# A pre-LN transformer block on one core: softmax without the row maximum, evacuations on VectorE, and a list-scheduled order

## The chip, the cores and the metric

The kernel runs on one core of one Trainium2 chip. The metric is the device time of one execution in microseconds (us). Times below are medians of several executions, with their range. Before the change the time was 1480.63 us (1480.35 to 1481.28, three runs).

Engines are named as in the profile: PE is TensorE (matrix products), PEld its weight loads, DVE is VectorE, ACT is ScalarE, POOL is GpSimd, SP is SyncE (it issues DMAs). `L1131` is a line of the kernel's source. The tile `pbank` in PSUM takes the results of the matmuls (`pbank<-...` in the traces); the kernels declare it as eight **banks** of 128x512 float32 each. A **dense** matmul is one of a projection or of the FFN, and **PV** is the product of the probabilities with the values.

## The reference

One block with S = 2048 tokens, D = 512, 32 heads of 16, and a gated FFN with F = 1792. All tensors are bf16, and the result may differ from the reference only by rounding. The code below is condensed by hand.

```python
def _A_ref(x, wqkv, wo):                       # attention, 32 heads of 16
    qkv = (x @ wqkv).reshape(B, S, 3, H, Dh).transpose(2, 0, 3, 1, 4)
    scores = einsum("bhqd,bhkd->bhqk", q, k) * (Dh ** -0.5)
    p = softmax(scores, axis=-1)
    return einsum("bhqk,bhkd->bhqd", p, v)...reshape(B, S, D) @ wo

def _B_ref(x, w_gate, w_up, w_down):           # gated FFN, tanh form of GELU
    return (gelu(x @ w_gate) * (x @ w_up)) @ w_down

h  = x + _A_ref(layernorm(x), A_wqkv, A_wo)
h2 = h + _B_ref(layernorm(h), B_w_gate, B_w_up, B_w_down)
```

The inputs are random with a scale of 0.05, so the scores are small numbers. That matters for a softmax that leaves out the maximum.

## The kernel before

Attention is cut into 32 **units**: 4 chunks of 512 queries times 8 slots of 4 heads. A unit has 32 ticks. In each tick TensorE makes two score tiles twice: once as queries x keys for the row maximum (pass 1, VectorE), and once transposed, as keys x queries with the negated maximum carried in extra rows, for the exponential (pass 2, ScalarE). The second pass runs one unit behind the first. Cuts are marked with `...`.

```python
def p1_pair(ui, j, gp, signal_last):                       # pass 1: scores for the maximum
    ...
    P.op("pe", lambda e, ...: e.matmul(pbank[:, b, :], QT[32*g:32*g+32, c, slot, 128*qt:128*qt+128],
                 KT[32*g:32*g+32, slot, 512*kc:512*kc+512], start=True, stop=True, tile_position=(32*g, 0)), ...)

def p1_consume(ui, tiles):                                 # 2048 of these, 128x512 each
    P.op("dve", lambda e, ...: e.tensor_reduce(out=PM[:, par, qt, kc, g:g+1], in_=pbank[:, b, :],
                                               axis=AX.X, op=ALU.max), ...)

def p2_consume(ui, tiles):                                 # 2048 of these, 128x512 each
    P.op("act", lambda e, ...: e.activation(out=PT[:, pi, :], in_=pbank[:, b, :], func=ACT.Exp), ...)

def evac_act(o_ap, i_ap, ...):                             # PSUM -> SBUF for projections, attention, FFN
    P.op("act", lambda e: e.activation(out=o_ap, in_=i_ap, func=ACT.Copy, **kw), ...)

def dummy(b, n):                                           # result is never read
    for i in range(n):
        P.op("pe", lambda e: e.matmul(pbank[:, b, :], ident[:], ones_bf[:, 0:512], start=True, stop=True), ...)

# ---- main loop, one pass per tick ----
    t1  = p1_pair(...)                     # 2 score matmuls for VectorE
    t2l = p2_pair(...)                     # 2 score matmuls for ScalarE
    p1_consume(...); p2_consume(...)
    pv_tick = p2_ok and (t2 % 4 == 1) and ...
    cost = 0 if pv_tick else dense.piece(deadline=dl)      # a piece (2 matmuls) of projection or FFN work
    if not pv_tick and (cost or 0) < 2 and p2_started:
        dummy(3 + p2_ring[0] % 3, 2 - (cost or 0))         # no dense work: multiply by ones instead
    if pv_tick:
        pv_burst(8)                        # probabilities x values
```

## Time and profile before

| quantity | before |
|---|---|
| time, median (range) | 1480.63 us (1480.35 to 1481.28) |
| span of the profiled execution | 1477.5 us |
| VectorE busy, ScalarE busy, TensorE busy | 88%, 87%, 75% |
| first exponential starts, last one ends | 94.6 us, 1411.5 us |
| tail after the last exponential | 66 us |
| start to start of two exponentials back to back, at best | 476 ns (each lasts 592 ns) |

The first fence holds lines of the profile's page of the kernel before. The first is busy time, share of the span and number of instructions of each engine. The second is the TensorE clock that the chip granted, in 40 equal slices, in tenths of full speed. The third is the share of the span that each engine holds in the chain of waits that ended last. The others are costly groups: line, engine, operation, output<-input, count, then busy us and mean ns of one, then the idle time before them and what ended it.

```profile
PE 1102.5 (75%) x8353; PEld 304.0 (21%) x8494; DVE 1301.6 (88%) x2159; ACT 1290.3 (87%) x2473; POOL 458.3 (31%) x593
...
PEclk9999999998999999999999999999999999999989
...
ACT 32%; DVE 31%; PE 19%; issue 16%; POOL 1%; DMA 1%; SPq 0%; POOLq 0%; ACTq 0%
...
L527 DVE TENSOR_REDUCE PM<-pbank 128x1 f32<-128x512 f32 x2048 | 1258.3, 683 | 70.7 <-PE pbank L568 56.2
L578 ACT ACTIVATE PT<-pbank 128x512 bf16<-128x512 f32 x2048 | 1117.8, 603 | 81.8 <-PE pbank L568 10.3
...
L810 PE MATMUL pbank<-ones_bf,ident 128*128 128x512 bf16 x756 | 239.9, 386 | 5.0 <-ACT PT L578 3.5
```

VectorE and ScalarE are both nearly full and share the chain. TensorE is not full, but it has 756 dummy matmuls, and its clock stands at full speed nearly throughout.

The second fence is from the timeline of the kernel before, in the middle of the run: start in us, length in us, then what ran.

```profile
700.43 0.39 PE L568 MATMUL pbank<-QT,KT 32*128 32x512 bf16 x2
...
700.75 0.61 PE L589 MATMUL pbank<-PT,VA 128*17 128x512 bf16 x8
...
701.29 0.39 PE L810 MATMUL pbank<-ones_bf,ident 128*128 128x512 bf16 x1
```

From the start of the score matmuls to the start of the next group is 0.32 us, and from the eight PV matmuls to the next group 0.54 us. Dense matmuls that follow each other are about 0.216 us apart; the score matmuls of a group start 3 ns apart, and so do four PV matmuls, with the next four some 0.21 us later. Each change of form costs about 0.1 us.

### The profile page before, as it was taken

To read this page: it belongs to the slowest core of one execution; us is meant where nothing else is said; L and a number is where in the kernel's file an instruction comes from. 1 tells how busy PE (TensorE), PEld (TensorE's weight loads), DVE (VectorE), ACT (ScalarE), POOL (GpSimd) and SP (SyncE) were. 2 spreads that over 40 slices of the span, in tenths; PEclk is the share of its full clock that TensorE was granted. 3 is DMA by queue.
4 is the path that set the end of the run, shared out by engine and by line. 5 is a ranking of instruction groups with operands and counts; after the bars stand their busy time and mean duration, and the time that the engine had idled before them with its cause. 6 is when DMAs were issued, how large, how long until landed. Compare 5 with 4: busy or idle time off the path is not lost.

```text
span 1477.5 us, 24601 instructions
## 1 busy us (share of the span) xinstructions
PE 1102.5 (75%) x8353; PEld 304.0 (21%) x8494; DVE 1301.6 (88%) x2159; ACT 1290.3 (87%) x2473; POOL 458.3 (31%) x593
## 2 busy tenths in 40 slices
PE   4977777776777777777887777777877777777869
PEld 2311111111112211111222211111222211111224
DVE  5989999998999999999999999999999999998023
ACT  3459999997999999999999999999999999999941
POOL 6000011110112245555212345554112345555130
PEclk9999999998999999999999999999999999999989
DMA  3000000013000000000000000000000000000000
GB/s 114 1 1 2 1 2 2 1 40 112 1 16 1 1 2 2 1 1 2 4 14 14 2 1 2 1 1 1 7 25 1 2 1 2 2 1 2 8 22 16
DMA packets 11531, 15.88 MB, mean 11 GB/s; under 512 B 1040, under 2 KB 9872, under 8 KB 11408
## 3 DMA queue, kind: packets, MB, share of 16 engines
q1 hardware_dynamic: 11408, 14.29, 2.9%
q8 instruction: 71, 1.16, 0.3%
q14 instruction: 52, 0.43, 0.1%
HBM read 11.80 MB, written 2.10 MB: 9 GB/s over the span
## 4 chain that ended last, share of the span: by engine, by line
ACT 32%; DVE 31%; PE 19%; issue 16%; POOL 1%; DMA 1%; SPq 0%; POOLq 0%; ACTq 0%
DVE PM L527 30%; ACT PT L578 27%; PE pbank L518 12%; PE pbank L794 2%; PE pbank L568 1%; PE pbank L462 1%; PE pbank L751 1%; ACT OA L440 1%; PE pbank L770 1%; ACT u_sb L440 1%; DVE stats L315 1%; ACT g_sb L440 1%; ACT sqj L682 0%; ACT OnT L440 0%; ACT QT L440 0%
## 5 line engine op out<-in xcount | busy, mean ns | idle before, releaser
L527 DVE TENSOR_REDUCE PM<-pbank 128x1 f32<-128x512 f32 x2048 | 1258.3, 683 | 70.7 <-PE pbank L568 56.2
L578 ACT ACTIVATE PT<-pbank 128x512 bf16<-128x512 f32 x2048 | 1117.8, 603 | 81.8 <-PE pbank L568 10.3
L518 PE MATMUL pbank<-KT,QT 32*128 32x512 bf16 x2048 | 399.5, 384 | 311.9 <-DVE PM L527 162.3
L568 PE MATMUL pbank<-QT,KT 32*128 32x512 bf16 x2048 | 398.1, 386 | 4.6 <-ACT PT L578 4.3
L518 PEld LDWEIGHTS pbank<-KT,QT 32*128 32x128 bf16 x2048 | 105.0, 91 | 776.3 <-DVE PM L527 767.6
L810 PE MATMUL pbank<-ones_bf,ident 128*128 128x512 bf16 x756 | 239.9, 386 | 5.0 <-ACT PT L578 3.5
L612 POOL TENSOR_TENSOR LINV<-OAT,negone 128x16 f32<-128x16 f32 x32 | 93.2, 2913 | 332.4 <-ACT OAT L440 332.4
L589 PE MATMUL pbank<-PT,VA 128*17 128x512 bf16 x2048 | 156.6, 383 | 0.0
L538 POOL CAST ST<-NEGM 128x16 bf16<-128x16 f32 x32 | 8.1, 252 | 358.1 <-DVE NEGM L532 358.1
L568 PEld LDWEIGHTS pbank<-QT,KT 32*128 32x128 bf16 x2048 | 96.2, 91 | 23.1 <-ACT PT L578 22.6
L729 POOL TENSOR_TENSOR w_sb<-g_sb 128x512 f32<-128x512 f32 x42 | 43.6, 1039 | 136.4 <-ACT g_sb L440 136.4
L810 PEld LDWEIGHTS pbank<-ones_bf,ident 128*128 128x128 bf16 x814 | 52.3, 97 | 110.6 <-ACT PT L578 96.4
L794 PE MATMUL pbank<-wd_sb,GUT 128*128 128x512 bf16 x214 | 57.0, 382 | 3.6 <-issue 1.0
L783 POOL TENSOR_TENSOR GUT<-th_sb,u_sb 128x512 bf16<-128x512 f32 x42 | 53.1, 1265 | 14.3 <-ACT u_sb L440 13.1
L802 DVE CAST out_sb<-pbank 128x512 bf16<-128x512 f32 x5 | 3.5, 692 | 61.2 <-PE pbank L798 61.2
L731 POOL TENSOR_TENSOR w_sb<-w_sb,g_sb 128x512 f32<-128x512 f32 x42 | 53.2, 1267 | 3.5
L735 POOL TENSOR_TENSOR th_sb<-th_sb,g_sb 128x512 f32<-128x512 f32 x42 | 53.2, 1266 | 3.5
L589 PEld LDWEIGHTS pbank<-PT,VA 128*17 128x17 bf16 x2048 | 28.3, 87 | 58.7 <-issue 58.4
L438 ACT ACTIVATE KT<-pbank,kbias 128x512 bf16<-128x512 f32 x32 | 22.1, 689 | 20.0 <-PE pbank L462 20.0
L462 PE MATMUL pbank<-xnT,wk_pad 128*128 128x512 bf16 x122 | 36.6, 415 | 1.9 <-issue 0.6
L462 PE MATMUL pbank<-xnT,wq_pad 128*128 128x512 bf16 x114 | 35.0, 383 | 2.3 <-issue 2.1
L734 POOL TENSOR_SCALAR th_sb<-th_sb 128x512 f32<-128x512 f32 x42 | 25.9, 618 | 28.6 <-ACT th_sb L741 28.6
(120 smaller groups left out, 749.7 us busy)
## 6 DMA issues: line engine op xcount, KB each, us to landing
x_sb<-in_A_x_dram SPq DMA_DIRECT2D x4, 512.0 KB, 5.6
QT<-STG SPq DMA_DIRECT2D x128, 3.0 KB
xres<-in_A_x_dram SPq DMA_DIRECT2D x16, 128.0 KB, 2.2
out_dram<-out_sb SPq DMA_DIRECT2D x16, 128.0 KB, 1.7
wg_sb<-in_B_w_gate_dram SPq DMA_DIRECT2D x1, 1792.0 KB, 7.1
wu_sb<-in_B_w_up_dram SPq DMA_DIRECT2D x1, 1792.0 KB, 11.2
wd_sb<-in_B_w_down_dram SPq DMA_DIRECT2D x1, 1792.0 KB, 16.8
wqkv_sb<-in_A_wqkv_dram SPq DMA_DIRECT2D x1, 1536.0 KB, 10.4
```

What stands on the lines that cost most here:

```text
L462: P.op("pe", lambda e, dc=dc: e.matmul(pbank[:, b, :], wp[:, dc, slot, :], xnT[:, dc, 512 * c:512 * c + 512], start=(dc == 0), stop=(dc == ...
L518: P.op("pe", lambda e, g=g, b=b: e.matmul(pbank[:, b, :], QT[32 * g:32 * g + 32, c, slot, 128 * qt:128 * qt + 128], KT[32 * g:32 * g + 32, ...
L527: P.op("dve", lambda e, b=b, qt=qt, kc=kc, g=g: e.tensor_reduce(out=PM[:, par, qt, kc, g:g + 1], in_=pbank[:, b, :], axis=AX.X, op=ALU.max ...
L568: P.op("pe", lambda e, g=g, b=b: e.matmul(pbank[:, b, :], KT[32 * g:32 * g + 32, slot, 128 * kt:128 * kt + 128], QT[32 * g:32 * g + 32, c, ...
L578: P.op("act", lambda e, b=b, pi=pi: e.activation(out=PT[:, pi, :], in_=pbank[:, b, :], func=ACT.Exp), reads=[("pb", b)], writes=[("PT", pi)])
L589: P.op("pe", lambda e, g=g, kt=kt, pi=pi, slot=slot: e.matmul(pbank[32 * g:32 * g + 17, PVB, :], VA[:, kt, 4 * slot + g, :], PT[:, pi, :], ...
L612: P.op("pool", lambda e: e.tensor_tensor(out=li, in0=oat4[:, :, :, 16], in1=negone[:].rearrange("p (q g) -> p q g", g=4), op=ALU.pow), rea ...
L731: P.op(eng, lambda e: e.tensor_tensor(out=ws, in0=ws, in1=gs, op=ALU.mult), reads=[("w", par), ("g", par)], writes=[("w", par)])
L735: P.op(eng, lambda e: e.tensor_tensor(out=ts_, in0=ts_, in1=gs, op=ALU.mult), reads=[("th", par), ("g", par)], writes=[("th", par)])
L783: P.op("pool", lambda e: e.tensor_tensor(out=GUT[:, fc, :], in0=ts_, in1=us, op=ALU.mult), reads=[("th", par), ("u", par)], writes=[("GUT" ...
L794: P.op("pe", lambda e, fc=fc: e.matmul(pbank[:, b, :], GUT[:, fc, 128 * qt:128 * qt + 128], wd_sb[:, fc, :], start=(fc == 0), stop=False), ...
L810: P.op("pe", lambda e: e.matmul(pbank[:, b, :], ident[:], ones_bf[:, 0:512], start=True, stop=True), reads=["ident", "ones_bf"], writes=[( ...
```

## The change

Intent: softmax does not need the maximum if the exponentials stay in range. So make the scores once, take the exponential directly, and check the sums at the end on chip: all 1/sum must lie between 1e-18 and 1e18. If one does not, the whole old algorithm runs behind a branch. That removes VectorE's main load, so the evacuations move from ScalarE to VectorE. Two exponentials merge into one of 128x1024. The order of all instructions comes from a list scheduler that works with a modelled duration for every operation.

The diff has about 2,100 lines. The old program stays in it as `max_path`. The core:

```diff
+# fast_path
+def qk():                                   # one step = two score tiles in two neighbouring banks
+    for st in range(NSTEP):                 # 1024 steps, two slots of two banks in turn
+        yield Op("pe", 0.25, [MM(pbank[:, bk[g % 2], :], KT[32*g:..., 128*kt:...], QT[32*g:..., c, slot, :],
+                                 True, True, (32*g, 0)) for g in (2*gp, 2*gp+1)],
+                 ..., gate=lambda: C["exp"] >= st - 1)
+def exps():
+    for st in range(NSTEP):
+        yield Op("act", 0.9, ACTF(PT[:, p0:p0+2, :], pbank[:, bk[0]:bk[0]+2, :], ACT.Exp), ...)
+def pv():                                   # every second step, four matmuls
+        yield Op("pe", 0.28, [MM(pbank[32*g:32*g+17, PVB, :], VA[:, kt, 4*slot+g, :], PT[:, p0+g, :],
+                                 kt == 0, kt == NT-1, (0, 32*g)) for g in range(4)], ...)
+def proj_kq(items):                         # dense pieces of two matmuls; FFN likewise
+    for hf in range(2):
+        yield Op("pe", 0.44, [MM(pbank[:, b, :], wp[:, dc, slot, :], xnT[:, dc, ...], dc == 0, dc == 3)
+                              for dc in (2*hf, 2*hf+1)], ...)
+    op = Op("dve", 0.61, lambda e, ...: e.tensor_copy(out=KT[...], in_=pbank[:, b, :]), ...)
+def check():                                # 1/sums in [1e-18, 1e18] -> flag == 128
+    ...
+        # every engine, at its end:
+            r = h.alloc_register("flag_" + name)
+            h.reg_load(r, flag[0:1, 0:1])
+            with h.If_ne(r, 128):
+                FP.run(name, h)             # max_path, the old algorithm
-    P.op("dve", lambda e, ...: e.tensor_reduce(out=PM[...], in_=pbank[:, b, :], axis=AX.X, op=ALU.max), ...)
-    P.op("pool", lambda e: e.tensor_tensor(out=li, in0=oat4[:, :, :, 16], in1=negone..., op=ALU.pow), ...)
-    dummy(3 + p2_ring[0] % 3, 2 - (cost or 0))
```

Only 26 dummy matmuls at the very start remain (`warm()`). An instruction still waits on its own engine's semaphore when it writes a bank that its own engine wrote last.

## The prediction

> **What bounds it now.** Span 1477.5 us; the profile's head shows VectorE busy 88%, ScalarE 87%, TensorE 75%. By costliest groups: the row-maximum reduction reads 2048 score tiles (128x512), 1258.3 us on VectorE; the exponential reads a second, transposed copy of the same scores in 2048 instructions, 1117.8 us on ScalarE. The chain of waits is shared: ScalarE 32%, VectorE 31%, TensorE 19%. In the trace two reductions start 598 ns apart, so one tick (two tiles of each pass) is about 1.2 us and 1024 ticks are 1225 us. Two exponentials fit in a tick with only ~0.2 us left for ScalarE's evacuations (about 170 us in all). First exponential at 94.6 us, last ends at 1411.5, then a 66 us tail.
>
> **Removed.** All 2048 reductions, 2048 score matmuls, maximum plumbing (32 transposes, copies, 128 small DMAs), 756 dummy matmuls, the 60 us of first pass before the first exponential, POOL's power with -1 (32 x 2.9 us). **Moved.** Projection, attention and FFN evacuations from ScalarE to VectorE: estimated from 0.69 us per evacuation, VectorE drops to about 250-300 us busy. **Merged.** Two exponentials become one of 128x1024: 1024 instructions. **Added.** 42 tanh remain on ScalarE; a tiny check and a branch on every engine; the old program, skipped (scores here are small, so I expect the branch not taken).
>
> **New bound: ScalarE's exponential stream.** Back-to-back 128x512 exponentials start 476 ns apart at best (592 ns each, overlapping), even when one carries an already satisfied wait. [...] 1024 steps = 925 us.
>
> Is TensorE in time? From the trace: exponential's end to score matmul 155 ns, matmul 390 ns, to the next exponential ~50 ns; with two slots a pair needs 1.02 + 0.6 = 1.62 us of 1.81, so ~0.19 us slack. A dense piece of two matmuls (0.43 us) fits between, so only occasional stalls.
>
> Sum (estimates):
> - start to first exponential 17 us
> - first unit, short of TensorE and VectorE time (projections, V, transposes ~38 us in a 29 us unit): 12 us of stall
> - exponentials 925, tanh 42 x 0.48 = 20
> - stalls of ScalarE from tanh waiting on POOL and from delayed score matmuls: 25
> - tail: ~62 (before 66; 28 gate/up groups of 0.86 us, four down groups of 3.0 us stay TensorE-bound; power of -1 leaves)
> - branch and offset between span and time: 3
>
> Total about 1064 us, i.e. -28%. Range 1035 to 1110. Chances: faster 0.97, same 0.01, slower 0.02.
>
> **What would show it.** Right: ScalarE busy over 88% and leading the chain (over 60%); exponential group 1024 x ~1.02 us, start-to-start 0.90; VectorE under 30%, TensorE 55-65%; first exponential near 17 us, last end near 1000. Wrong in a step: exponentials starting ≥0.95 us apart with "idle before" owed to the score matmul (slack missed) or to VectorE via a bank; ScalarE idle before tanh, released by POOL, over 10 us; tail over 70 us; first unit over 45 us.
>
> **What would make it wrong.** Without dummy matmuls TensorE's granted clock may fall below full in stretches without projection or FFN work: a score matmul then takes ~0.2 us longer, the slack is gone and each step grows (a few per cent; upper end of the range). The order is fixed ahead from modelled durations; where real latencies are longer, in-order waits on banks can cascade into ScalarE. A 1024-wide read across two PSUM banks costing more than estimated adds 10 us per 10 ns. If the check failed, the old program would run too: about 2500 us.

The sum is 17 + 12 + 925 + 20 + 25 + 62 + 3 = 1064 us. The 925 is 1024 steps of 0.903, and the kernel after shows that step: 903 ns from start to start at best, each 1018 to 1023 ns long. The clock that the last paragraph names as a risk is in the trace of after as well: 0.50 in the stretch 210 to 310 us, with 0.604 us for a score matmul in place of 0.384.

## The result, and the profile after

The time is 1198.99 us (1195.56 to 1202.32, four runs). The ratio to before is 0.810 (95% interval 0.8078 to 0.8121). Ratios here are the mean time of one kernel's fast runs over that of the other's in the same rounds, so they are not quite the ratio of the medians quoted. The kernel is correct and the branch is not taken. It is much faster, as predicted, but 135 us slower than the predicted time and 89 us above the top of the range.

The lines of the page of the kernel after that answer to those of before:

```profile
PE 1072.0 (90%) x5442; PEld 268.1 (22%) x5499; DVE 277.8 (23%) x478; ACT 1019.5 (85%) x1102; POOL 189.5 (16%) x194
...
PEclk9799998555799955555589955555569965555589
...
PE 65%; issue 14%; ACT 14%; DVE 2%; POOL 1%; ACTq 0%; DVEq 0%
...
L1131 ACT ACTIVATE PT<-pbank 128x1024 bf16<-128x1024 f32 x1024 | 983.5, 1023 | 99.0 <-PE pbank L1125 86.7
L1125 PE MATMUL pbank<-QT,KT 32*128 32x512 bf16 x2048 | 526.0, 519 | 80.7 <-ACT PT L1131 59.8
...
L1418 DVE SCALAR_TENSOR_TENSOR w_sb<-w_sb,g_sb 128x512 f32<-128x512 f32 x42 | 41.9, 999 | 7.4 <-ACT w_sb L1417 7.3
```

Three readings follow. First, TensorE does fewer matmuls than before (5442 against 8353) and yet is busy for 90% of the span and holds 65% of the chain; ScalarE, the predicted bound, holds 14%. (Some matmul records are missing from the trace; the weight loads, 5499 against 8494, are the better count.) Second, long stretches of the clock line read 5: TensorE ran at half speed there. Third, a score matmul takes 519 ns on average. Told apart in the trace, that is 0.384 us at full clock and 0.604 us at half clock.

Next, the windows view of the kernel after, three stretches: start:end and length in us, then busy us and number of instructions of each engine, the granted clock (PEclk, 1.00 is full), the DMA share and GB/s.

```profile
core 0: us, PE busy (x) PEld busy (x) DVE busy (x) ACT busy (x) POOL busy (x), PEclk, DMA share, GB/s
100.00:195.00 95.00, 92.51 (x552) 25.60 (x562) 35.34 (x55) 89.77 (x93) 0.00 (x0) 1.00 0.01 2
210.00:310.00 100.00, 87.96 (x425) 19.51 (x422) 5.39 (x12) 95.21 (x101) 0.00 (x0) 0.50 0.01 2
370.00:400.00 30.00, 28.16 (x166) 8.02 (x169) 11.62 (x17) 26.87 (x31) 9.64 (x9) 1.00 0.03 10
```

The first stretch has projections and full clock. The second is **quiet**, which here means that attention is the only work: half clock, with TensorE shown as 88% busy. The third is FFN work at full clock: TensorE is busy for 28.16 of 30 us. A high busy share alone doesn't make it the limit (it is 88% in the second stretch too); which wait holds ScalarE there is read from the timeline below.

Unit by unit, from the start of a unit's first exponential to that of the next unit (an ideal unit is 32 x 0.903 = 28.9 us):

| part | predicted | measured | difference |
|---|---|---|---|
| start to the first exponential | 17 | 26.0 | +9.0 |
| unit 0, above 28.9 | 12 | 18.6 | +6.6 |
| units 1 to 4 (projections), above 28.9 each | 0 | 15.4 | +15.4 |
| 18 quiet units, above 28.9 each | 0 | 49.6 | +49.6 |
| 9 units with FFN work, above 28.9 each (tanh 20 + stalls 25) | 45 | 88.8 | +43.8 |
| tail | 62 | 70.8 | +8.8 |
| sum | | | +133.2 |

So the spacing of the exponentials, 903 ns at best (925 us in all), is as predicted, and the miss is ScalarE waiting. In the profiled execution the sum accounts for the whole difference to the prediction (1195.56 - 1064 = 132; the prediction's last 3 us are for the branch and the offset between span and time).

Two places of the timeline show how ScalarE comes to wait. The first is a quiet unit of the kernel after:

```profile
242.33 0.61 PE L1125 MATMUL pbank<-QT,KT 32*128 32x512 bf16 x2 [0.55 <-ACT PT L1131]
...
243.25 0.61 PE L1125 MATMUL pbank<-QT,KT 32*128 32x512 bf16 x2 [0.31 <-ACT PT L1131]
243.79 0.60 PE L1125 MATMUL pbank<-PT,VA 128*17 128x512 bf16 x4
...
244.32 0.61 PE L1125 MATMUL pbank<-QT,KT 32*128 32x512 bf16 x2
```

With two slots, a slot's loop is the exponential (1.02), 0.16 to the score matmuls, 0.61 for them, and 0.05 to the next exponential: 1.84 us for two steps. Two steps of ScalarE need 1.81, so at half clock the slack is already gone. In one of two loops the score matmuls also stand behind a PV group (243.79), which holds them back by about 0.15 us more. The result is 1.98 us for two steps. At full clock the loop is 1.02 + 0.16 + 0.38 + 0.05 = 1.61 us and fits.

The second is a unit with FFN work, at full clock:

```profile
375.33 0.39 PE L1125 MATMUL pbank<-QT,KT 32*128 32x512 bf16 x2
...
375.65 0.40 PE L1125 MATMUL pbank<-PT,VA 128*17 128x512 bf16 x4
...
375.98 1.27 PE L1124 MATMUL pbank<-hnT_c_70,wu_sb 128*128 128x512 bf16 x4
...
376.64 0.11 PEld L1124 LDWEIGHTS pbank<-hnT_c_70,wu_sb 128*128 128x128 bf16 x2 [0.55 <-PE pbank L1124]
377.18 0.10 PEld L1125 LDWEIGHTS pbank<-QT,KT 32*128 32x128 bf16 x4 [0.42 <-ACT PT L1131]
...
377.61 1.02 ACT L1131 ACTIVATE PT<-pbank 128x1024 bf16<-128x1024 f32 x1 [0.52 <-PE pbank L1125]
```

Score to PV is 0.32 us and PV to dense 0.33 us. Then two dense pieces stand directly behind each other, and the second waits for the first to end: the weight load at 376.64 is released by PE itself. The four matmuls take 1.27 us, and the next exponential starts 0.52 us after ScalarE had become free. Across the trace a dense pair costs 0.54 us (median) until the next group starts, not 0.43.

The start is the third place, again from the timeline of the kernel after:

```profile
1.74 17.28 PE L1486 MATMUL pbank<-ones_bf,ident 128*128 128x512 bf16 x26 [1.74 <-POOL ident L1156]
...
12.53 0.56 DVE L1175 COPY wk_pad<-wqkv_sb 128x1536 bf16<-128x1536 bf16 x1 [3.00 <-DMA wqkv_sb<-in_A_wqkv_dram]
...
16.08 8.27 POOL L1214 TENSOR_SCALAR xn_sb<-x_sb,mv,rstd 128x512 bf16<-128x512 bf16 x4 [0.19 <-POOL rstd L1209]
```

Each of the 26 warm-up matmuls waits for the one before (0.667 us each, modelled as 0.25) and so they hold TensorE until about 19 us. On VectorE a copy waits 3.00 us for a load before it can start, and so does what stands behind it. POOL's four normalisations take 2.07 us each, modelled as 0.77. In before four of the same shape took 0.77 us, but these multiply and add, and after's subtract and multiply; VectorE is not the reason, since the first of the four took 2.09 us with VectorE idle throughout.

### The profile page after: what moved, and what is told of

Read it like the earlier page. It is cut to its first block, busy times and chain, and to the rows that moved or that the text cites. A ratio compares the mean times of both kernels' runs of the same rounds, so it can differ in the third digit from the quotient of the medians.

```text
span 1193.7 us, 14797 instructions
## 1 busy us (share of the span) xinstructions
PE 1072.0 (90%) x5442; PEld 268.1 (22%) x5499; DVE 277.8 (23%) x478; ACT 1019.5 (85%) x1102; POOL 189.5 (16%) x194
## 4 chain that ended last, share of the span: by engine, by line
PE 65%; issue 14%; ACT 14%; DVE 2%; POOL 1%; ACTq 0%; DVEq 0%
PE pbank L1125 39%; PE pbank L1124 20%; ACT PT L1131 13%; PE pbank L1323 3%; PE pbank L1365 2%; DVE OA L1319 1%; POOL xn_sb L1214 1%; PE pbank L1359 0%; PE pbank L1381 0%; ACT w_sb L1417 0%; ACTq L152 0%; DVE stats_93 L1372 0%; DVE w_sb L1418 0%; DVE QT L1254 0%; DVE h_c_69 L1368 0%
## 5 line engine op out<-in xcount | busy, mean ns | idle before, releaser
L1131 ACT ACTIVATE PT<-pbank 128x1024 bf16<-128x1024 f32 x1024 | 983.5, 1023 | 99.0 <-PE pbank L1125 86.7
L1125 PE MATMUL pbank<-QT,KT 32*128 32x512 bf16 x2048 | 526.0, 519 | 80.7 <-ACT PT L1131 59.8
L1125 PE MATMUL pbank<-PT,VA 128*17 128x512 bf16 x2048 | 270.1, 519 | 0.8 <-ACT PT L1131 0.6
L1323 PE MATMUL pbank<-ident_79,OA 128*128 128x128 f32 x128 | 38.9, 401 | 6.5 <-DVE OA L1319 5.7
L1418 DVE SCALAR_TENSOR_TENSOR w_sb<-w_sb,g_sb 128x512 f32<-128x512 f32 x42 | 41.9, 999 | 7.4 <-ACT w_sb L1417 7.3
L1407 DVE COPY g_sb<-pbank 128x512 f32<-128x512 f32 x42 | 29.0, 690 | 35.9 <-PE pbank L1124 35.8
L1443 DVE SCALAR_TENSOR_TENSOR GUT<-pbank,w_sb 128x512 bf16<-128x512 f32 x42 | 29.0, 691 | 24.5 <-PE pbank L1124 23.2
L1410 POOL TENSOR_SCALAR w_sb<-w_sb 128x512 f32<-128x512 f32 x42 | 30.5, 726 | 3.7
L1257 DVE CAST KT<-pbank 128x512 bf16<-128x512 f32 x32 | 22.1, 691 | 31.6 <-PE pbank L1124 31.6
L1365 PE MATMUL pbank<-wo_sb,OnT 128*128 128x512 bf16 x57 | 24.9, 529 | 2.6 <-issue 1.7
L1417 ACT ACTIVATE w_sb<-w_sb 128x512 f32<-128x512 f32 x42 | 26.3, 626 | 0.0
## 6 DMA issues: line engine op xcount, KB each, us to landing
wu_sb<-in_B_w_up_dram SPq DMA_DIRECT2D x1, 1792.0 KB, 11.8
```

The costliest lines, as they stand in the source:

```text
L1125: return lambda e: e.matmul(o, l, r, start=start, stop=stop, tile_position=tile)
L1131: return lambda e: e.activation(out=o, in_=i, func=func, **kw)
L1323: yield Op("pe", 0.44, [lambda e, qt=qt: e.transpose(out=pbank[:, b, 128 * qt:128 * qt + 128], in_=OA[:, par, 128 * qt:128 * qt + 128], id ...
L1365: yield Op("pe", 0.44, [lambda e, hc=hc: e.matmul(pbank[:, b2, :], OnT[:, qt, hc, :], wo_sb[:, hc, :], start=(hc == 0), stop=(hc == 3)) fo ...
L1407: yield Op("dve", 0.61, lambda e: e.tensor_copy(out=gs, in_=pbank[:, b, :]), reads=[("pb", b)], writes=[("g", i)], extra=dE)
L1410: yield Op("pool", 0.62, lambda e: e.tensor_scalar(out=ws, in0=ws, scalar1=GA, scalar2=1.0, op0=ALU.mult, op1=ALU.add), reads=[("w", i)], ...
```

## The experiments

Three theories at the outset:

- **Clock:** without dummies TensorE falls to half clock in the quiet units, and this lengthens the loop beyond ScalarE's time. Holding the clock gives the time back.
- **Groups and self-waits:** at full clock TensorE is still late, because a change of matmul form and TensorE's waits on its own semaphore cost time that the scheduler's model leaves out.
- **POOL (rival):** in the FFN units ScalarE's tanh waits for the three POOL operations of GELU.

15 kernels ran. "Quiet units" are the 18 units without dense work, `QUIET = [5, 6, 7]` and the last five of each later chunk. A run of a program on one core is labelled slow when it is more than 1.5% above the fastest of the same kernel; here every such run shows a lower mean clock than the fast ones of its kernel (spreadT 0.81 and 0.85 against 0.91 to 0.92). The profiles of fill2noself, spread, spreadfill and spreadT are of executions labelled slow: unit times quoted for them hold for those executions, and the fast ones may have lost the clock in other places. Ratios are to the kernel before, of fast runs only. They ran in four groups (1 to 4, 5 to 8, 9 to 12, 13 to 15), each on one chip of its own; the kernel before measured about 1480 us in each.

### 1. fill2: two dummy matmuls per two steps in the quiet units

```diff
                 C["pv"] = n
+                if u in QUIET and kt % 1 == 0:
+                    b = yield Acquire(reads=["ones_bf", "ident"])
+                    yield Op("pe", 0.44, [MM(pbank[:, b, 0:512], ident[:], ones_bf[:, 0:512], True, True)] * 2, ...)
+                    sch.release(b)
```

> Two 128x512 dummy matmuls (identity times ones, into a free bank) after each PV group in the 18 units that have no projection or FFN work; the order on ScalarE, VectorE and POOL is unchanged. Theory A (clock): those units run at granted clock 0.5, where the loop exponential - score matmul - exponential takes 1.02+0.16+0.61+0.05 = 1.84 us per pair plus 0.15 us behind a PV group, so 0.99 us per step; with the clock back at 1.0 these units fall from 31.7 to 29.0-29.5 us, the units after them start warm, in all -45 to -65 us (about 1135-1150 us). Rival B (in-order waits on TensorE, whatever the clock): extra TensorE work can only lengthen the step; same or up to 30 us slower.

Measured: 1153.98 us (1143.42 to 1154.46), ratio 0.7774 (0.7737 to 0.7812), clock 0.952 on average against 0.70. ScalarE, VectorE and POOL have the same instructions in the same order as after. The clock line of the page of fill2, then from its windows view a quiet stretch and an FFN stretch:

```profile
PEclk9899999699999979999989979999989979999989
...
250.00:300.00 50.00, 42.21 (x269) 11.87 (x274) 1.41 (x4) 50.00 (x56) 0.00 (x0) 1.00 0.00 1
360.00:390.00 30.00, 28.19 (x163) 7.70 (x166) 14.61 (x20) 26.82 (x31) 14.34 (x13) 1.00 0.01 5
```

TensorE has more matmuls than in the quiet stretch of after (5.4 per us against 4.25), is busy for less of the time (84% against 88%), and ScalarE is busy for 50.00 of 50 us. A quiet unit takes 29.6 us in place of 31.7. The gain has two halves. The 18 quiet units together save 20 us, because each group's first one still starts at half clock (33.5 to 34.9 us). The units that follow them, 8, 16 and 24, no longer start at half clock and save 19 us (37.6, 43.3, 43.1 become 33.2, 36.1, 36.1). Units 9 and 10 do not change. The clock theory is confirmed for some 45 us, and its rival (more TensorE work can only lengthen a step) is out. The first unit of a group pays for the change: unit 11 takes 33.6 us where it took 31.4, since it has the dummies before it has the clock.

### 2. fill1: half the dose

The same edit with one matmul in place of two.

> The same with one dummy matmul per PV group (half the dose). Theory A: if one is enough to hold the clock, the same gain as with two, -45 to -65 us; if the clock stays at 0.5 in those units, the extra matmul (0.43 us at half clock) delays every second score matmul and it is 10-60 us slower. Rival B: between 0 and 15 us slower, with no jump.

Measured: 1267.8 us (1262.63 to 1272.68), ratio 0.8578. The windows view of fill1, a quiet stretch:

```profile
260.00:300.00 40.00, 36.18 (x167) 8.42 (x166) 1.37 (x3) 33.73 (x37) 0.00 (x0) 0.50 0.00 1
```

The clock stays at half, and the dummy is now pure cost: +69 us, with quiet units at 34.8 to 36 us. This is the outcome that was named for a clock that stays at half, and more than the 10 to 60 us expected for it. So there is no smooth trade: 0.22 us of extra streaming per two steps (at full clock) did not hold the clock, 0.43 us did. TensorE is 90% busy in this stretch and is still not given the full clock.

### 3. noself: TensorE does not wait for itself

The waits on TensorE's own semaphore are left out. The result was correct in the run.

```diff
-            if k == e.name and v > e.count:
+            if k == e.name and (v > e.count or k == "pe"):
                 continue
```

> TensorE's waits on its own semaphore are left out ([...]inside a group there were none before either). Order of all engines unchanged. Theory: the second half of each dense piece waits for the first half's drain (0.55 us against 0.43 us of work), so back-to-back halves lose ~0.2 us; in the tail 24 of them fall: gates and ups 2.04 us per pair to 1.75, tail -4 us; in the FFN units 2-4 us per unit, 9 units; in all -15 to -35 us. Rival: halves seldom stand back to back outside the tail, so only the tail's 4-5 us come.

Measured: 1170.48 us (1165.76 to 1179.61), ratio 0.7924. The tail falls from 70.8 to 60.7 us, unit 9 from 40.5 to 38.6, and quiet units from 31.7 to 31.1. The self-waits cost about 27 us, within the 15 to 35 expected, but not where they were expected. In the profiles 10 us are in the tail and 13 in the 18 quiet units, which run at half clock; the nine FFN units, for which 2 to 4 us each were expected, give back 2.5 us together, because units 18 and 26 lost the clock for a while (34.4 became 37.2 and 35.7). The self-waits account for the miss in the tail.

### 4. nopool: POOL's GELU made almost empty

Wrong (relative error 0.024): the three POOL operations work on one column, and tanh reads another tensor.

```diff
-        yield Op("pool", 1.05, lambda e: e.tensor_tensor(out=ws, in0=gs, in1=gs, op=ALU.mult), ...)
+        yield Op("pool", 1.05, lambda e: e.tensor_tensor(out=ws[:, 0:1], in0=gs[:, 0:1], in1=gs[:, 0:1], op=ALU.mult), ...)
         ... (the other two likewise)
-        yield Op("act", 0.5, lambda e: e.activation(out=ws, in_=ws, func=ACT.Tanh, scale=GC), ...)
+        yield Op("act", 0.5, lambda e: e.activation(out=ws, in_=gs, func=ACT.Tanh, scale=GC), ...)
```

> Wrong results on purpose: POOL's three GELU operations work on 1 column instead of 512, tanh reads the gate values directly; order and waits unchanged. Rival C (the FFN units, 34-43 us against 28.9, are held by POOL's chain, which runs 1.19+0.73+1.35 us instead of 1.04+0.62+1.27, and by VectorE's slowed SBUF operations): each FFN unit falls by 4 us or more, in all -35 us or more. Theory A2 (FFN units are held by TensorE: dense pieces cost 0.54 us not 0.43 and push the score matmul past its slack): less than 8 us in all.

Measured: 1200.68 us (1194.36 to 1201.84), ratio 0.8104, the same as after. The FFN units are unchanged (37.6, 40.4, 34.4 us). POOL is not the limit, and this rival is out. (The start and unit 0 took 6 us more in this profile, at a lower clock: the third slice of its clock line is 8, in after 9.) One line changed, in the groups view of nopool:

```profile
L1418 DVE SCALAR_TENSOR_TENSOR w_sb<-w_sb,g_sb 128x512 f32<-128x512 f32 x42 | 28.8, 686 | 7.4 <-ACT w_sb L1417 7.3
```

This VectorE operation took 999 ns on average in after (679 to 1796) and takes 686 ns in nopool, where POOL is nearly idle. Overlap with POOL alone does not set the time: some of those in after took under 700 ns with POOL busy beside them almost throughout.

### 5. fill2narrow: FFN matmuls of half the width

fill2, with gate, up and down matmuls of 256 columns. Its output is wrong, which doesn't matter for the time. If TensorE's time in the FFN units is the limit, they should shrink.

```diff
-                yield Op("pe", 0.44, [MM(pbank[:, b, :], wg_sb[:, dc, ...], hT[:, dc, :], dc == 0, dc == 3)
+                yield Op("pe", 0.44, [MM(pbank[:, b, 0:256], wg_sb[:, dc, ...], hT[:, dc, 0:256], dc == 0, dc == 3)
```

> Wrong results on purpose, on top of fill2 (clock held): gate, up and down matmuls stream 256 columns instead of 512; order and waits unchanged. Theory A2 (the second FFN unit of each chunk, 40.4 us, is held by TensorE's own streaming: 85 dense matmuls x 0.216 + scores and PV 10.4 us + ~80 changes of group x 0.1 us = 37 us): it falls by about 85 x 0.108 = 9 us to 31-32 us, the third unit from 34.4 to 29.5-30.5, and the tail by 10-18 us; in all -45 to -65 us against fill2 (about 1090-1105 us). Rival (latency of waits between engines, not streaming): the second unit falls by less than 4 us.

Measured: 1196.96 us (1196.09 to 1198.27), ratio 0.8086: 45 us slower than fill2, not 45 to 65 faster. The windows view of fill2narrow, the same place as the second line of fill2 above:

```profile
360.00:400.00 40.00, 38.91 (x173) 9.26 (x171) 15.82 (x24) 29.31 (x34) 19.44 (x18) 0.50 0.00 1
```

With less work to stream, TensorE fell to half clock in units 9 and 10 and they took 51.3 and 44.1 us in place of 40.4 and 34.4. The experiment cannot answer the question it was made for, and whether TensorE's own streaming is the limit of the FFN units stays without a test. It shows something else: with less work for TensorE the kernel became slower, and the units that grew are those where the clock went.

### 6. fill2noself: both together

> fill2 and noself together, to see whether they add up. If independent: fill2's 1149 us less 15-25 us (tail -10, FFN units -1.5 each; the 0.6 us per quiet unit that noself gained at half clock is not there at full clock): 1125-1135 us. If noself's gain came through the clock, only the tail's 10 us: 1140 us.

The edits of 1 and 3. Measured: median 1139.3 us; one fast run of 1118.86 at clock 0.964, and three labelled slow (1137.5 to 1141.2, clock 0.933 to 0.941), so there is no ratio. In the profiled run quiet units take 29.4 us, unit 9 38.4, and the tail 60 us. Against fill2's mean of 1151.5 the fast run gains 33 us and the others 10 to 14, so the two gains add up in one run of four only. The profile shows where it goes: units 17, 18, 25 and 26, which held the full clock in fill2, now dip below it (0.97 and 0.91; 40.1 and 37.2 us for the first two). Why they dip is not shown.

### 7. spread: the scheduler gets measured durations

noself, with the durations that the trace showed and a guard that keeps a dense piece from starting if it would delay the next score matmuls by more than 0.15 us. No dummies.

```diff
+EXTRA = dict(pe=0.06, act=0.19, dve=0.09, pool=0.05)     # from an operation's end to its user
+SLACK = 0.15
-            yield Op("pe", 0.25, [MM(...)])               # score group;  PV 0.28 -> 0.33, dense 0.44 -> 0.54
+            yield Op("pe", 0.33, [MM(...)])
+            qr = self._qk_due()                           # when the next score matmuls can start
+            if "pe" in best and qr < self.INF: ...        # push a dense piece that does not fit behind them
```

> noself, and the list scheduler given the measured durations (score group 0.33, PV 0.33, dense pair 0.54 us) and a guard: a dense pair may not start when it would end more than 0.15 us after the next score group is due; so FFN work spreads over 7 units per chunk (10-38 dense matmuls per unit, before 85 in one). No dummies. Theory A2: no unit after the first is over 32 us, FFN units 29.5-31 at full clock; [...] in all 1065-1090 us. Rival (total work, not its bunching): the units' sum stays, about 1165 us as noself.

Measured: 1204.94 us (1186.71 to 1227.32; the two fast ones average 1194.4), ratio 0.807. Expected were 1065 to 1090, so this missed by over 100 us. Against noself (fast mean 1171.8), which it contains, it is 23 us slower. Two stretches of the windows view of spread:

```profile
120.00:240.00 120.00, 117.02 (x465) 21.36 (x472) 18.64 (x30) 96.73 (x95) 0.00 (x0) 0.50 0.00 1
470.00:520.00 50.00, 43.33 (x265) 11.45 (x270) 12.72 (x20) 50.00 (x58) 14.63 (x15) 1.00 0.00 1
```

Both stretches have about 28 dense matmuls per unit, evenly spread. In the first, units 2 to 5 run at half clock throughout and take 40.6 us each. In the second the clock is full, ScalarE is busy for 50.00 of 50 us, and the units take 29.3 to 31.6 us. The even order does what it was made for, but only at full clock. A load of about 28 dense matmuls per unit can stay in either state for over 100 us, so the number of matmuls alone does not decide. Whether the state in which it was entered does, or the order within the units, no run isolates.

### 8 to 10. spreadfill, spreadT, spreadTP: dummies only where TensorE would be slack

spreadfill adds a dummy pair after a PV group if no dense pair ran since the PV group before:

```diff
+                if C["warm"] and C["dense"] == C["dense0"]:
+                    b = yield Acquire(reads=["ones_bf", "ident"])
+                    yield Op("pe", 0.54, [MM(pbank[:, b, :], ident[:], ones_bf[:, 0:512], True, True)] * 2, ...)
```

> As spread, with a pair of dummy matmuls after a PV group whenever the last period had no dense pair (never more than one pair per period). Theories A and A2 together: every unit after the first at 29.3-30.3 us at clock 0.95 or more; 26 us start + 46 first unit + 31 x 29.8 + 61 tail = 1050-1065 us. If the clock costs nothing once the work is spread: the same as spread.

Measured: 1178.53 us (1149.77 to 1198.26; fast mean 1158.3), ratio 0.7826. Missed (1050 to 1065 expected). In the profile the clock is at 0.58 to 0.73 in units 4 to 6, 8, 14 to 16, 22 to 24, 26, 28 and 31. The working guess was that transposes are the cause, since the edit counts a transpose group as dense work and leaves the dummies out there. The profile does not show it: every unit has transposes, and units 3 and 4 have nearly the same matmuls, one at full clock and one at 0.58.

spreadT does not count transposes, puts a 256-column dummy matmul ahead of each group of them, and adds a dummy pair only where no dense work is waiting:

```diff
-        yield Op("pe", 0.5, [lambda e, hc=hc: e.transpose(out=pt[...], in_=Otok[...], identity=ident[:]) for hc in range(4)], ...)
+        yield Op("pe", 0.60, [MM(pbank[:, b, 0:256], ident[:], ones_bf[:, 0:256], True, True)]
+                           + [lambda e, hc=hc: e.transpose(...) for hc in range(4)], ...)
```

> As spreadfill, but a transpose group no longer counts as a dense pair (in spreadfill it suppressed the dummies, and its periods had no 512-column matmul) and carries one 256-column dummy itself; a dummy pair comes only when no dense work waits. So every PV period (1.8 us) has about two full matmuls or one half-wide one. Theory A3 [...]: clock 0.93 or more, units after the first 29.3-31 us, in all 1050-1080 us. Rival: the clock is unstable at this load whatever the gaps: 1130 us or more.

Measured: 1125.63 us (1119.58 to 1198.52; three of five fast, mean 1122.0), ratio 0.7566. Expected were 1050 to 1080: missed. In the profile, of a slow execution (1171.01), the later units are mostly at full clock, but units 2 to 5 still take 40.9 us at half clock. The fast runs have a clock of 0.91 to 0.92 against 0.85; where they lost it was not profiled.

spreadTP also mends the start: LayerNorm on VectorE in place of POOL, longer landing times of the loads in the schedule (6 to 9 us) and the warm-up matmul at 0.43 us.

> spreadT with the start reordered: real landing times of the loads in the schedule, the normalised input on VectorE instead of POOL, the warm-up dummies modelled at their real 0.43 us. Expected: first exponential at 18-22 us instead of 26-32, first unit 40-46 us, so -8 to -15 us against spreadT if the clock does the same in both.

Measured: 1181.68 us (1167.81 to 1209.12; fast mean 1170.9), ratio 0.7982: some 49 us slower than spreadT, where 8 to 15 us less were expected. The first exponential comes at 27.5 us in place of 32.0, but the clock was at or near half in units 2 to 5 again and in 16, 17, 24 and 25 as well (0.55 to 0.67). So a small shift at the start came with a different set of units that lose the clock. The four runs with the new order agree on one thing: as long as the clock was lost somewhere, the gain of the order was not reliable.

### 11. zeropv: other matmuls in place of the dummies

Which matmuls keep the clock: only dummies of the form 128\*128, as in fill2, or others that stream for as long? Eight more PV-shaped matmuls (form 128\*17) with zero weights after each PV group in the quiet units, accumulating zeros. In the trace of before eight PV matmuls take 0.54 us until the next group, as a dense pair does, so they are taken to stream for 0.43 us, like fill2's pair.

```diff
-                                      for g in range(4)],
+                                      for g in range(4)]
+                         + ([MM(pbank[32*g:32*g+17, PVB, :], zw[:, 0:17], PT[:, p0+g, :], False, False, (0, 32*g))
+                             for g in range(4)] * 2 if u in QUIET and kt < NT - 1 else []),
```

> Change as it came, plus after each PV group of the quiet units two more PV-shaped groups with zero weights (17 columns in each of 4 column groups): the same 0.43 us of streaming per period as fill2, in narrow matmuls. If the clock follows streaming time: as fill2, -45 us (1150). If it follows the share of the array in use: clock stays 0.5 and the extra groups (0.86 us at half clock) hold up the scores: +40 to +80 us (1240-1280).

Measured: 1162.84 us (1160.62 to 1164.75), ratio 0.7851, clock 0.941. A quiet stretch in its windows view:

```profile
250.00:280.00 30.00, 24.18 (x258) 7.29 (x260) 1.38 (x3) 29.76 (x33) 0.00 (x0) 1.00 0.01 1
```

It holds the clock nearly as well as fill2 (0.952); in the profile it lost it once in unit 8, which takes 44.9 us in place of 33.2, about the 11 us that lie between the means of the two. So neither the form 128\*128 nor non-zero weights were needed: 0.43 us more of streaming per two steps was enough in either form, and fill1's 0.22 was not.

### 12. evacact: evacuations back on ScalarE

fill2, with 185 evacuations on ScalarE as before the change.

```diff
-        yield Op("dve", 0.61, lambda e: e.tensor_copy(out=OA[:, par, :], in_=pbank[:, PVB, :]), ...)
+        yield Op("act", 0.5, lambda e: e.activation(out=OA[:, par, :], in_=pbank[:, PVB, :], func=ACT.Copy), ...)
```

> fill2 with the plain PSUM evacuations (K, Q, V, attention output, both transposes, gate; 185 in all) back on ScalarE. If ScalarE's stream is the bound: 185 x 0.476 = 88 us more, less what falls into its waits for TensorE in the FFN units: 1195-1240 us. If TensorE is the bound nearly everywhere: under 25 us more.

Measured: 1332.81 us (1330.33 to 1337.88), ratio 0.8998: +181 us against fill2's mean of 1151.5, where 45 to 90 were expected. ScalarE's busy time grows by 104 us (1111.0 against 1007.1), and the clock falls to 0.80. The list scheduler also made another order: the trace has at most 4 dense matmuls left in units 9 and 10 (clock 0.5 to 0.55), and 22 to 36 in each of units 12 to 15, beside the dummies that stay there (38 to 41 us each at a clock over 0.9). So the 181 us are three things, the move, the clock, and dummies standing beside dense work, and no run separates them. That stays open.

### 13 to 15. spreadU, spreadU3, fill2noselfP: closing the sum

spreadU is spreadTP without the guard in the first five units (so that projections come early; in after the clock is 1.00 beside them, from 100 to 195 us), with landing times of the loads nearer to the measured ones (7 to 13.5 us), and with 512 columns of dummy beside each transpose group.

```diff
-            if "pe" in best and qr < self.INF:
+            if "pe" in best and qr < self.INF and self.C["exp"] >= 32 * 5:
-        yield Op("pe", 0.60, [MM(pbank[:, b, 0:256], ident[:], ones_bf[:, 0:256], True, True)] + [... transposes ...], ...)
+        yield Op("pe", 0.56, [MM(pbank[:, b, :], ident[:], ones_bf[:, 0:512], True, True)] + [... transposes ...], ...)
```

> spreadTP without the guard in the first five units (their bunched projections held the clock in the change as it came), with 512 columns of dummy beside each transpose group. Theory A3: clock 0.95 or more, units 1 to 4 about 32-33 us, the rest 29.3-32; start 20 + first unit 45 + 4 x 32.5 + 27 x 30.3 + tail 61 = 1070-1085 us. If the clock still falls at chunk starts (units 8, 16, 24): 1100-1130.

Measured: 1067.8 us (1063.15 to 1070.66), ratio 0.7203, clock 0.97 to 0.98. Unit 0 takes 36.7 us, units 1 to 4 29.3 each. Only units 17 and 25 still lose the clock for a longer while (35.2 and 36.1 us; units 6 and 22 dip to 0.94).

spreadU3 uses three dummies where spreadU uses two:

```diff
-                    yield Op("pe", 0.54, [MM(pbank[:, b, :], ident[:], ones_bf[:, 0:512], True, True)] * 2, ...)
+                    yield Op("pe", 0.76, [MM(pbank[:, b, :], ident[:], ones_bf[:, 0:512], True, True)] * 3, ...)
```

> spreadU with three dummies instead of two in an empty period. If the margin of the clock is what fails at chunk starts, the higher dose holds it: 1065-1085 us and smaller spread between runs than spreadU. If two are enough: the same as spreadU within 10 us; the dose itself costs nothing (1.75 us of TensorE in a period of 1.81).

Measured: 1066.62 us (1065.21 to 1067.39), ratio 0.7205 (0.7193 to 0.7217), clock 0.99. It is correct, and faster than both kernels. The time is that of spreadU; the third dummy bought a steadier clock and a smaller spread. Lines of the page of spreadU3:

```profile
PE 958.9 (90%) x5950; PEld 279.5 (26%) x5950; DVE 273.2 (26%) x490; ACT 984.6 (92%) x1102; POOL 155.2 (15%) x182
...
PEclk8999999999999999999999999999999999999989
...
ACT 55%; PE 30%; issue 12%; DVE 1%; DMA 0%; POOL 0%; ACTq 0%; SPq 0%; POOLq 0%; DVEq 0%
```

The windows view of spreadU3, the same FFN stretch as for fill2:

```profile
360.00:390.00 30.00, 26.66 (x166) 7.42 (x164) 9.93 (x16) 30.00 (x37) 11.92 (x13) 1.00 0.00 1
```

And the waits of ScalarE's exponential on the score matmul (line and engine waiting <- what ended it: us in all, number of waits, longest), first of after, then of spreadU3:

```profile
ACT PT L1131 <- PE pbank L1125: 86.7, 136, 6.0
```

```profile
ACT PT L1159 <- PE pbank L1153: 11.8, 3, 5.1
```

ScalarE is busy for 30.00 of 30 us even in the FFN stretch, and its waits on the score matmul fall from 86.7 us in 136 waits to 11.8 us in 3. Every unit after the first takes 29.1 to 31.9 us. ScalarE leads the chain now, with 55%. TensorE runs some 450 more matmuls than after (5950 weight loads against 5499), for 113 us less of busy time.

fill2noselfP tells the start and the clock apart from the order: it is fill2noself with the mended start, but with the original order and model.

> fill2noself with only the start reordered (real landing times of the loads, the normalised input on VectorE instead of POOL, warm-up dummies at 0.43 us each). First exponential at 17-20 us instead of 25.5-27, first unit 45-49: 6-9 us less than fill2noself at the same clock (1119 at clock 0.964, 1139 at 0.933).

Measured: 1112.75 us (1104.82 to 1118.04), ratio 0.7500. The first exponential comes at 21.5 us (17 to 20 expected) and unit 0 takes 41.7 us (45 to 49 expected). In spreadU3, which has the same edits of the start in another order of instructions, they are 26.0 and 36.7 us, so the sum of the two is the same within 0.6 us.

The chain of gains: after 1199; clock held in the quiet units (fill2) 1154; self-waits removed and start mended (fill2noselfP) 1113; order made with measured durations and the clock held everywhere (spreadU3) 1067. The last step changes two things at once, the order and the placing of dummies, and no run separates them at full clock. spread, with the order alone on top of noself, lost 23 us.

## Why the prediction was right or wrong, point by point

**Right: the exponential.** One of 128x1024 takes 1018 to 1023 ns and back to back they start 903 ns apart; the prediction said 1.02 us and 903 ns. It had no trace for the slope when it was made; before and after together now show it: (1018 - 592) / 512 = 0.832 ns per element. Two in a row overlap by 592 - 476 = 116 ns at 512 elements and by 1018 - 903 = 115 ns at 1024. VectorE under 30% busy (23%), the branch not taken, and the direction were right too.

**Wrong: "A dense piece of two matmuls (0.43 us) fits between, so only occasional stalls".** This step failed, and it is two terms of the sum: 12 us for the first unit and 25 us of stalls elsewhere, 37 in all. Measured are 172 us above the ideal units less 20 for tanh, so 152. In the terms of the prediction, the slack of ~0.19 us was taken with a score matmul of 390 ns and dense work of 0.43 us. Two causes:

- *The size at full clock.* A dense pair costs 0.54 us until the next group, a score group 0.32, and half a PV group 0.16 per step: 1.02 us where ScalarE needs 0.903. The prediction counted streaming time only. This is read from the traces; the run made to test it (fill2narrow) lost the clock. The missing 0.1 us per change of form was in the trace of before (700.43 to 700.75 us above). It falls between scores (form 32\*128), PV (128\*17) and dense matmuls (128\*128); at half clock it is there too, with 0.53 us from a score group to PV in after, where two dense matmuls are 0.40 to 0.43 us apart. (Within a form the next matmul follows after 0.21 to 0.23 us even when another tile is read: in before it is 0.215 to 0.217 us, 30 times, from an output-projection or FFN matmul to the identity matmul on `xres` or `h_c`.) Waits of TensorE on itself add little to it at full clock (noself, 2.5 us in the nine FFN units). What adds most is that the dense work stands close together: up to 88 dense matmuls fall into one unit, and spreadU3, with the same dense matmuls spread out (at most 38 in a unit with FFN work) and the clock held, needs 31.9 us at most for such a unit.
- *The clock.* At half clock a score matmul takes 604 ns and the loop is over ScalarE's budget (1.84 us against 1.81). The clock records of after hold 0.5 and 1.0 alone, and the longest stretches at 0.5 last 195 us; in the quiet stretch shown (210 to 310 us) TensorE is 88% busy and waits for 0.6 us at most. The prediction named this risk as "a few per cent; upper end of the range", but its sum has it at 0. The size was not far off: holding the clock in the quiet units gave 45 us (fill2), and 1064 + 45 = 1109 is the upper end of the range. An estimate with all 18 quiet units at fill2's 29.6 us gives 57 (18 x 2.1, and 19 in the units that follow). So the clock alone took the time to about the top of the range, and the rest came from the first cause, the start and the tail. Before has hardly a stretch at half clock, and it has 756 dummies, which the prediction listed under "removed" and not as a loss; that they hold the clock there (0.99) is inference from fill2, and no run took them out of before.

**Wrong in size: start (17 predicted, 26.0 measured) and tail (62, 70.8).** The start lost time to warm-up matmuls that waited on themselves, to loads that landed later than modelled, and to POOL. With these mended the first exponential came at 21.5 us (fill2noselfP), but at 26 to 27 us in the other order (spreadU, spreadU3), so the three causes are named from the timeline and their shares are not shown. The tail's term was right once the self-waits were gone (60.7 in noself).

**Falsified signs of the prediction's own list.** It said that ScalarE would be over 88% busy and lead the chain with over 60%: 85% and 14%. TensorE would be 55 to 65% busy: 90%. Half clock stretches its work (88% in a quiet stretch with 4.25 matmuls per us), but the share is no less at full clock (90% in spreadU3, with more dummies), so it is no measure of the miss. It also gave the signs of failure, "exponentials starting ≥0.95 us apart with idle before owed to the score matmul": that is what came. So did two others, a tail over 70 us (70.8) and a first unit over 45 us (47.5). POOL ahead of tanh, also listed, did not come (nopool).

**With the failing step mended, the sum holds, in part by luck.** spreadU3, whose ScalarE is hardly held up any more, takes 1066.6 us; the sum said 1064. Term by term its profile has 26.0 us for the start (17 predicted), 7.8 above the ideal in unit 0 (12), 43.3 in the other units with tanh (45), and 62.5 for the tail (62). The stalls and the tail are as the sum said; the start is still 9 us late, and the shorter unit 0 makes up for half of that. One thing is unexplained: its exponentials start 903 ns apart at best as before, but the page shows 1223 ns for one on average.

**Open:** the exact rule by which the clock is lost and won back; how evacact's +181 us divide; whether the dummies held the clock in before; why the clock was lost where it was in spread to spreadTP; and the share of order and of dummies in the last 46 us.

## What to carry to other kernels

Before removing work that looks useless from an engine with slack, ask what it holds up: here two idle-looking dummy matmuls per two steps kept TensorE at full clock (1.00 in the quiet stretch of fill2, 0.50 in that of after), and twice a kernel with less work for TensorE was slower than fill2 (fill1 by 116 us, fill2narrow by 45). When the new bound is an engine with a two-slot loop, write the loop out at full and at half clock and compare both with the budget of a step (here 1.61 and 1.84 us against 1.81 for two steps); if only the first fits, hold the clock by design and not by chance. Take group costs from start to start of different groups in the trace, not from the streaming rate within one, and give a list scheduler those numbers, but hold the clock first: with the clock lost, the better order gained nothing here.
